# Two-layer transform kernel: the odd part accumulates onto the even part in one PSUM bank, VectorE forms only the difference, one round later

## The chip, the cores and the metric

One core of a Trainium2 chip runs the whole program. The metric is the device time of one execution in microseconds, from the first to the last instruction and the little that lies around it. Three executions of the kernel before gave 2941.29, 2942.25 and 2944.97 us, so the time to beat is the median, 2942.25 us. The engines are named as the profile names them: PE is TensorE's matmul (PEld its weight load), DVE is VectorE, ACT is ScalarE, POOL is GpSimd, SP is SyncE, whose queue issues most transfers.

## The reference

The input `x` is 8 x 3072 x 256. Three layers follow one another, cut here to what matters:

```
X = fft(fft(x, axis=1), axis=2).real          # 24576 tokens of width 256
h = X @ w_in            (256 -> 2048)
y = (h - tanh(h)) @ w_out   (2048 -> 256)
h2 = y @ w_in2          (256 -> 1024)
s = h2 * softmax(h2)
out = layernorm(s) * g_ln @ w_out2   (1024 -> 256)
```

All of it is float32.

## The kernel before, in words

A first stage (about the first 160 us) does the transform along the sequence and leaves, for each batch, an even part and an odd part in device memory. The transform along the width is folded into `w_in`: `fold_w_in` (L385 to L412) makes weights `wt` with two parts, one for the even and one for the odd part of a token. A token and its mirrored partner share these parts: with a = even part + (middle row) and b = odd part, the token's hidden value is a + b and the partner's is a - b. The middle row is one extra number per token, `nu`, kept in device memory as `nu_d`, with weights `wnu`. Row 0 of the odd part carries no data; `low` inside `fold_w_in` clears its weights with a memset on POOL (L410).

The main stage is a loop over steps (L1149), 48 groups of 512 tokens by 16 blocks of 128 hidden units, so 768 steps; the document calls a step a **round**. Each float32 product is three passes with split operands (high x high, high x low, low x high), so three matmuls. In round (n, m), before the change:

- PE: `ab` (L871) makes the even part and the odd part side by side in one PSUM tile `ab` (six matmuls of 256 columns), pool `p_ab`, two banks.
- DVE: `lead` (L886) makes `asb` = nu * wnu + even part; `act_in` (L893) then writes `asb` + odd part (L900) and `asb` - odd part (L901) into a PSUM tile `h` (pool `p_h`, one bank). ACT takes tanh of `h` into `t` (L907).
- One round later, `act_out` (L910): DVE subtracts, t = h - t (L912); ACT rounds the result to the high part `gh` and POOL takes the rest as its low part (helpers at L166 and L169, which also split `xs`, `ut` and `zs`).
- Two rounds later, `o1` (L919): six matmuls of 512 columns add `gh` times `w_out` into `x2p` (L927).

Interleaved with this, a second layer runs on pairs of 128-token tiles, one pair in eight rounds. `layer2` (L1095) keeps, for three places in a round ("ahead", "early", "late"), a list of works with the round in which each is due, counted from the pair's first round by `pair_at` (L1091). The document numbers these rounds **0 to 7**, one **period**. What matters here:

- Round 0, "ahead": PE makes a first block product in `bank_a`, ACT copies `bank_a` to `bank_b` (L1099). Round 0, "late": PE adds another product to `bank_a`, so it must wait for that copy.
- Round 1, "ahead": a product is added to `bank_b` and ACT keeps it in SBUF (`kept`, L971); "late": a further product is added to `bank_b`, after that copy.
- Round 4: products into `bank_b` (early) and `bank_a` (late). Round 5, "ahead": DVE takes `bank_a` with a running minimum (`block`, L978); "late": PE adds a further product to `bank_a`, after that read.
- Round 6: a DVE `block`. Rounds 7 and 0: the two `weigh` operations of DVE (L1002), with two SBUF inputs. Rounds 1 and 3: transposes through device memory (`turn`). Rounds 2, 3, 6 and 7: PE's output products `po` (`outp`), eight matmuls each.

The periods alternate, since a group has 16 rounds. In one, DVE forms four sums of blocks of the previous group (`sum_x2`, L943) in rounds 6 and 7: the **S-period** of this document. In the other, ACT and POOL split the next group's input `zs` near the same place: the **Z-period**. Both end with a round 0 and its copy. All engines work through their queues in the order of the program (`manual_schedule`); nothing reorders them.

## Time and profile before

| what | value |
|---|---|
| median of three executions | 2942.25 us |
| the profiled execution, its own time | 2943.85 us |
| its span, first to last instruction | 2942.1 us |
| PE busy / DVE busy / POOL busy / ACT busy | 93% / 88% / 77% / 71% |
| mean granted TensorE clock | 0.978 |
| DMA | 103 GB/s on average, 360 GB/s in the first slices |

The span is cut into stages by what runs there: the transform stage until about 160 us, the main loop until about 2900 us, and a tail of the last tiles. In the 40 slices of the page every engine has nearly the same busy share throughout the main loop. Times of single instructions are durations by the profiler; where two instructions follow on one engine, the document also uses the distance of their starts, since ends overlap. A remark like "[0.78 <-ACT bank_b L1099]" behind a row says that the engine idled 0.78 us just before, and what released it.

### The profile page before, as it was taken

What the parts mean: (1) busy time and instruction counts of PE and PEld (TensorE: products, weight loads), DVE (VectorE), ACT (ScalarE), POOL (GpSimd) and SP (SyncE); (2) the same over time, 40 slices, a digit from 0 to 9 for tenths busy, and PEclk for the clock granted to TensorE, in tenths of its full rate; (3) what the DMA queues carried; (4) which work ended last, traced back from release to release, by engine and by line L of the source; (5) the groups of instructions that cost most, each with busy time, mean ns of one, the idle gap of its engine ahead of it and who ended that gap; (6) DMA issues with size and microseconds to landing.
All of it is one profiled execution on the core that took longest, in us unless ns stands there. A gap on an engine that the chain in (4) does not pass through costs nothing.

```text
span 2942.1 us, 47965 instructions
## 1 busy us (share of the span) xinstructions
PE 2742.7 (93%) x15073; PEld 2364.6 (80%) x15073; DVE 2600.9 (88%) x4970; ACT 2098.6 (71%) x3990; POOL 2250.9 (77%) x2500
## 2 busy tenths in 40 slices
PE   9988999999999999999999999999999999999998
PEld 5667887888888788788888878888888888888887
DVE  8978898888988989888998889889888889888995
ACT  3556777777777777777777777777777777777776
POOL 0057887888888788888878888887887888888784
PEclk9999999999999999999999999999999999999999
DMA  9932333434334343443434434343443434334341
GB/s 360 362 117 47 91 94 85 101 83 98 85 89 100 84 95 86 94 94 81 100 85 96 93 85 96 85 95 87 92 95 84 101 82 98 87 87 101 82 97 47
DMA packets 882558, 302.97 MB, mean 103 GB/s; under 512 B 788496, under 2 KB 844048, under 8 KB 879008
## 3 DMA queue, kind: packets, MB, share of 16 engines
q1 hardware_dynamic: 879696, 293.40, 40.8%
q10 hardware_dynamic: 2304, 6.42, 0.6%
q8 instruction: 121, 1.98, 0.3%
...
## 4 chain that ended last, share of the span: by engine, by line
PE 37%; DVE 28%; POOL 14%; ACT 10%; issue 9%; DMA 2%; SPq 0%; POOLq 0%; DVEq 0%; ACTq 0%
PE x2p L927 12%; PE ab L877 7%; PE bank_a L956 5%; DVE asb L888 4%; DVE t L912 4%; DVE h L900 4%; DVE h L901 4%; PE bank_b L956 4%; DVE xb L943 3%; PE po L1060 3%; POOL ut L169 3%; DVE u L1002 3%; POOL gh L169 3%; DVE u L978 2%; POOL xs L169 2%
## 5 line engine op out<-in xcount | busy, mean ns | idle before, releaser
L927 PE MATMUL x2p<-gh,wo 128*128 128x512 f32 x4608 | 1150.4, 385 | 2.6 <-POOL gh L169 1.3
L169 POOL TENSOR_TENSOR gh<-t,gh 128x512 fp32r<-128x512 f32 x768 | 1000.3, 1305 | 130.4 <-ACT gh L166 113.5
L927 PEld LDWEIGHTS x2p<-gh,wo 128*128 128x128 f32 x4608 | 835.4, 192 | 141.5 <-POOL gh L169 35.9
L907 ACT ACTIVATE t<-h 128x512 f32<-128x512 f32 x758 | 452.9, 598 | 420.5 <-DVE h L901 322.0
L877 PEld LDWEIGHTS ab<-zs,wt 128*128 128x128 f32 x4608 | 650.4, 196 | 55.8 <-issue 12.1
L166 ACT ACTIVATE gh<-t 128x512 fp32r<-128x512 f32 x768 | 481.1, 626 | 264.0 <-DVE t L912 231.2
L877 PE MATMUL ab<-zs,wt 128*128 128x256 f32 x4608 | 656.6, 280 | 11.1 <-DVE bank_b L901 9.6
L912 DVE TENSOR_TENSOR t<-h,t 128x512 f32<-128x512 f32 x758 | 514.4, 679 | 107.5 <-ACT t L907 80.9
L169 POOL TENSOR_TENSOR ut<-um,ut 128x512 fp32r<-128x512 f32 x372 | 497.5, 1338 | 81.7 <-ACT ut L166 44.4
L1060 PE MATMUL po<-wo,ut 128*128 128x512 f32 x1528 | 523.1, 383 | 0.8 <-DVE x2t L169 0.8
L956 PE MATMUL bank_a<-wi,xs 128*128 128x512 f32 x1128 | 325.8, 399 | 151.2 <-ACT bank_b L1099 150.3
L888 DVE SCALAR_TENSOR_TENSOR asb<-nb,wnu,ab 128x256 f32<-128x256 f32 x768 | 364.7, 475 | 106.3 <-PE ab L877 88.7
L1067 PE MATMUL po<-wo,ut 128*128 128x256 f32 x1528 | 417.2, 273 | 0.0
L169 POOL TENSOR_TENSOR xs<-xb,xs 128x256 fp32r<-128x256 f32 (+1 forms) x282 | 241.4, 856 | 182.7 <-ACT xs L166 181.3
L956 PEld LDWEIGHTS bank_a<-wi,xs 128*128 128x128 f32 x1128 | 202.9, 193 | 210.5 <-ACT bank_b L1099 188.9
L901 DVE TENSOR_TENSOR h<-asb,ab 128x256 f32<-128x256 f32 x758 | 324.5, 428 | 26.1
L900 DVE TENSOR_TENSOR h<-asb,ab 128x256 f32<-128x256 f32 x758 | 324.6, 428 | 26.0
L1060 PEld LDWEIGHTS po<-wo,ut 128*128 128x128 f32 x1528 | 290.5, 190 | 31.6 <-DVE x2t L169 1.0
L1002 DVE SCALAR_TENSOR_TENSOR u<-u,e 128x1024 f32<-128x1024 f32 x188 | 312.9, 1664 | 0.0
L1067 PEld LDWEIGHTS po<-wo,ut 128*128 128x128 f32 x1528 | 293.9, 192 | 0.3 <-POOL ut L169 0.2
L956 PE MATMUL bank_b<-wi,xs 128*128 128x512 f32 x846 | 265.0, 412 | 18.6 <-POOL xs L169 7.5
L166 ACT ACTIVATE ut<-um 128x512 fp32r<-128x512 f32 x372 | 231.3, 622 | 23.5 <-DMA um<-mv_d 23.0
...
## 6 DMA issues: line engine op xcount, KB each, us to landing
...
```

What stands on the lines that cost most here:

```text
L166: nc.scalar.activation(out=o, in_=i, func=AF.Copy)
L169: eng.tensor_tensor(out=o, in0=i, in1=hi.bitcast(F32), op=ALU.subtract)
L877: nc.tensor.matmul(in_pairs(pab[:, u]), wt[c][:, hw, u, o : o + P], in_turn(zs[:, hz, u]), start=(i == 0), stop=(i == 2),)
L888: nc.vector.scalar_tensor_tensor(out=asb, in0=zg[n][1], scalar=wnu[:, m : m + 1], in1=pab[:, 0], op0=ALU.mult, op1=ALU.add)
L900: nc.vector.tensor_tensor(out=h[:, 0], in0=asb, in1=pab[:, 1], op=ALU.add)
L901: nc.vector.tensor_tensor(out=h[:, 1], in0=asb, in1=pab[:, 1], op=ALU.subtract)
L907: nc.scalar.activation(out=t, in_=h, func=AF.Tanh)
L912: nc.vector.tensor_tensor(out=g, in0=hs.pop((n, m)).rearrange("p u n -> p (u n)"), in1=g, op=ALU.subtract)
L927: nc.tensor.matmul(in_pairs(x2p[n][mt]), wo1[c][:, hw, k, mt * P : (mt + 1) * P], in_turn(gh[:, hg]), start=(m == 0 and i == 0), stop=(m = ...
L956: nc.tensor.matmul(in_pairs(bank), xs[:, hx, xs_at[a]], in_turn(wi2[:, b, hw]), start=(start and q == 0), stop=(q == 2), skip_group_check= ...
L1060: nc.tensor.matmul(in_pairs(po), ut[:, 0, ks], wo2[:, k].rearrange("p h x n -> p (x n) h"), start=(k == 0), stop=False,)
L1067: nc.tensor.matmul(in_pairs(po[:, :D]), ut[:, 1, ks], wo2[:, k, :, 0].rearrange("p h n -> p n h"), start=False, stop=(k == NK2 - 1),)
```

## The change

The odd part's row 0, empty before, now carries `nu` as data and keeps the weights of the middle row (the memset is gone). So the odd part's product contains nu * wnu. PE makes the even part into `h`'s first half, DVE makes `asb` = nu * wnu + even part from it, and only after that PE adds the odd part on top, in the same bank. The first half is then even + odd + nu * wnu, which is the token's value without a DVE operation, and DVE makes the partner's as 2 * asb - first half, with one scalar_tensor_tensor. `ab` and `p_ab` are gone; `p_h` has three banks in place of one. `parity(.., 1)` and `act_in` come one round after `even` and `lead`, so tanh, `act_out`, `o1` and all of the second layer come one round later too. For each of the 48 groups one DMA of 1 KB on SP brings `nu` into row 0 of `zc`.

```diff
         o = zc[n, u] = zp.tile([P, GP], F32, tag="zc", name=f"zc{n}_{u}")
         for _ in sums_of(eng, o, zf[:, u, 0], zf[:, u, 1], n % GPB - NSJ):
             pass
+        if u == 1:
+            b, g = divmod(n, GPB)
+            nc.sync.dma_start(out=o[0:1], in_=nu_d[b : b + 1, g * GP : (g + 1) * GP])
...
             yield rest(nc.vector, wt[c][:, 1], wf, wt[c][:, 0])
-            nc.gpsimd.memset(wt[c][0:1, :, 1].bitcast(F32), 0.0)
...
-    p_ab = pool(first, "p_ab", 2, space=PSUM)
-    p_h = pool(first, "p_h", 1, space=PSUM)
+    p_h = pool(first, "p_h", 3, space=PSUM)
...
+    def parity(n, m, u):
+        zs = zg[n][2]
         c, o = m // 4, (m % 4) * P
+        for i, (hw, hz) in enumerate(PASSES):
+            nc.tensor.matmul(
+                in_pairs(hs[n, m][:, 0]),
+                wt[c][:, hw, u, o : o + P],
+                in_turn(zs[:, hz, u]),
+                start=(u == 0 and i == 0),
+                stop=(i == 2),
+                skip_group_check=True,
+            )
+
+    def even(n, m):
+        if n == 0 and m % 5 > 2:
+            hs[n, m] = (bank_a, bank_b)[m % 5 - 3].rearrange("p (u n) -> p u n", u=2)
+        else:
+            hs[n, m] = p_h.tile([P, 2, GP], F32, tag="h", name=f"h{n}_{m}")
+        parity(n, m, 0)
...
-        nc.vector.tensor_tensor(out=h[:, 0], in0=asb, in1=pab[:, 1], op=ALU.add)
-        nc.vector.tensor_tensor(out=h[:, 1], in0=asb, in1=pab[:, 1], op=ALU.subtract)
+        h = hs[n, m]
+        nc.vector.scalar_tensor_tensor(
+            out=h[:, 1], in0=as_.pop((n, m)), scalar=2.0, in1=h[:, 0], op0=ALU.mult, op1=ALU.subtract
+        )
...
-        p, r = divmod(step - NM - 4 - back, 8)
+        p, r = divmod(step - NM - 5 - back, 8)
...
-    for step in range(steps + 2):
+    for step in range(steps + 3):
         n, j = divmod(step, NM)
         if step in at_ab:
             special(at_ab[step])
+        if 0 < step <= steps:
+            parity(*divmod(step - 1, NM), 1)
         if step < steps:
-            pab = ab(n, j)
-            asb = lead(n, j, pab) if n == 0 else None
-
-        lag = 2 if step < NM else 1
+            even(n, j)
+        if 0 < step <= steps:
+            act_in(*divmod(step - 1, NM))
+        lag = 3 if step < NM else 2
...
         layer2(step, "ahead")
         if step < steps:
-            act_in(n, j, pab, asb or lead(n, j, pab))
+            lead(n, j)
         if 0 < n < NG:
-            for blk in {2: (S1, S2, S3), 3: (S4,)}.get(j, ()):
+            for blk in {3: (S1, S2, S3), 4: (S4,)}.get(j, ()):
...
-        s1 = step - 4 if step < NM else step - 2
+        s1 = step - 5 if step < NM else step - 3
```

The order in which the engines get their work moves with it. DVE, rounds 6 and 7 of an S-period, in the kernel before (`t` is the result of `act_out`, `asb` of `lead`, `xb` the block sums, the ISA rows are `block`, `u71` with `e71` is `weigh`; a name's first two numbers are group and block):

```order
L912 TENSOR_TENSOR t19_1_13483<-h19_1_13480,t19_1_13483 128x512
L888 SCALAR_TENSOR_TENSOR asb19_2_13510<-nb19_12931,wnu_123,ab19_2_13499 128x256
L900 TENSOR_TENSOR h19_2_13512<-asb19_2_13510,ab19_2_13499 128x256
L901 TENSOR_TENSOR h19_2_13512<-asb19_2_13510,ab19_2_13499 128x256
L943 TENSOR_TENSOR xb_1232<-xb_1232 128x256 x3
L978 ISA u70_13309,st70_13310<-bank_a_1246,u70_13309,st70_13310 128x512
L978 ISA st70_13310 128x1
L912 TENSOR_TENSOR t19_2_13515<-h19_2_13512,t19_2_13515 128x512
```

And in the changed kernel:

```order
L901 SCALAR_TENSOR_TENSOR h19_2_12882<-asb19_2_12894,h19_2_12882 128x256
L913 TENSOR_TENSOR t19_1_12887<-h19_1_12850,t19_1_12887 128x512
L894 SCALAR_TENSOR_TENSOR asb19_3_12924<-nb19_12331,wnu_123,h19_3_12913 128x256
L944 TENSOR_TENSOR xb_1227<-xb_1227 128x256 x3
L979 ISA u70_12733,st70_12734<-bank_a_1241,u70_12733,st70_12734 128x512
L979 ISA st70_12734 128x1
L901 SCALAR_TENSOR_TENSOR h19_3_12913<-asb19_3_12924,h19_3_12913 128x256
L913 TENSOR_TENSOR t19_2_12918<-h19_2_12882,t19_2_12918 128x512
```

A round has three operations in place of four, and the round now begins with the difference, which needs this round's first matmuls; `t` of the block before stands behind it.

ACT, from the end of round 7 to the copy of round 0 (L1099 before, L1100 now), in the kernel before:

```order
L993 ACTIVATE e70_13564,st70_13310<-u70_13309,st70_13310 128x1024
L1077 ACTIVATE o2_68_13574<-po68_13525,st68_12984 128x512
L166 ACTIVATE xs_1233<-xb_1232 128x256
L166 ACTIVATE gh19_3_13598<-t19_3_13560 128x512
L1099 COPY bank_b_1247<-bank_a_1246 128x512
L907 ACTIVATE t19_4_13610<-h19_4_13607 128x512
```

And in the changed kernel:

```order
L994 ACTIVATE e70_12977,st70_12734<-u70_12733,st70_12734 128x1024
L1078 ACTIVATE o2_68_12987<-po68_12934,st68_12423 128x512
L166 ACTIVATE xs_1228<-xb_1227 128x256
L909 ACTIVATE t19_4_13005<-h19_4_12962 128x512
L166 ACTIVATE gh19_3_13008<-t19_3_12967 128x512
L1100 COPY bank_b_1242<-bank_a_1241 128x512
```

The tanh (`t` from `h`) moved from behind the copy to ahead of the rounding and the copy, in every round in which ACT copies a bank.

POOL, rounds 6 and 7 of a Z-period (`zs` the split of the next group's input), in the kernel before:

```order
L169 TENSOR_TENSOR gh19_9_13841<-t19_9_13819,gh19_9_13841 128x512
L1085 TENSOR_TENSOR o2_69_13754<-o2_69_13754 128x256
L169 TENSOR_TENSOR xs_1233<-xb_1232,xs_1233 128x256
L169 TENSOR_TENSOR gh19_10_13881<-t19_10_13849,gh19_10_13881 128x512
L169 TENSOR_TENSOR xs_1233<-xb_1232,xs_1233 128x256
L169 TENSOR_TENSOR zs20_13589<-zc20_0_13762,zs20_13589 128x256
L169 TENSOR_TENSOR zs20_13589<-zc20_1_13765,zs20_13589 128x256
```

And in the changed kernel:

```order
L169 TENSOR_TENSOR gh19_9_13240<-t19_9_13208,gh19_9_13240 128x512
L1086 TENSOR_TENSOR o2_69_13160<-o2_69_13160 128x256
L169 TENSOR_TENSOR xs_1228<-xb_1227,xs_1228 128x256
L169 TENSOR_TENSOR zs20_12958<-zc20_0_13118,zs20_12958 128x256
L169 TENSOR_TENSOR zs20_12958<-zc20_1_13121,zs20_12958 128x256
L169 TENSOR_TENSOR gh19_10_13282<-t19_10_13237,gh19_10_13282 128x512
L169 TENSOR_TENSOR xs_1228<-xb_1227,xs_1228 128x256
```

The split of `zs` is tied to the block number 11, everything of the second layer to the round; so `zs` now stands one round earlier against the second layer, ahead of the low part of `gh` of round 7.

## Rows read from the trace of the kernel before

**Rows 1.** PE's timeline, a Z-period's hold (start us, us, engine, line, operation, count)

```profile
1504.81 1.46 PE L927 MATMUL x2p<-gh,wo 128*128 128x512 f32 x6
1507.04 0.92 PE L956 MATMUL bank_a<-wi,xs 128*128 128x512 f32 x3 [0.78 <-ACT bank_b L1099]
1507.79 0.83 PE L877 MATMUL ab<-zs,wt 128*128 128x256 f32 x6
...
1509.11 1.46 PE L927 MATMUL x2p<-gh,wo 128*128 128x512 f32 x6
1510.41 0.81 PE L956 MATMUL bank_b<-wi,xs 128*128 128x512 f32 x3
```

**Rows 2.** PE's timeline, the next S-period's hold, and the next Z-period's

```profile
1527.31 0.83 PE L877 MATMUL ab<-zs,wt 128*128 128x256 f32 x6
...
1530.58 0.83 PE L877 MATMUL ab<-zs,wt 128*128 128x256 f32 x6
...
1531.90 1.46 PE L927 MATMUL x2p<-gh,wo 128*128 128x512 f32 x6
1535.71 0.92 PE L956 MATMUL bank_a<-wi,xs 128*128 128x512 f32 x3 [2.35 <-ACT bank_b L1099]
...
1563.48 0.91 PE L956 MATMUL bank_a<-wi,xs 128*128 128x512 f32 x3 [0.78 <-ACT bank_b L1099]
```

**Rows 3.** The instructions of line 1099: duration min/median/max, first and last start

```profile
L1099 ACT COPY bank_b<-bank_a x94: 576/580/678, 224.1 to 2871.8; 128x512 f32<-128x512 f32 x94
```

**Rows 4.** A window behind another hold: busy PE, PEld, DVE, ACT, POOL, granted clock, DMA

```profile
910.50:912.00 1.50, 1.50 (x7) 1.41 (x7) 1.44 (x4) 0.40 (x1) 1.50 (x1) 0.50 0.00 0
```

**Rows 5.** Waits of PEld: us in total, times, longest us

```profile
PEld bank_b L956 <- POOL xs L169: 37.7, 66, 1.0
...
PEld bank_b L956 <- ACT u L971: 15.0, 23, 1.6
```

**Rows 6.** DVE's timeline, rounds 6, 7 and 0 of the S-period

```profile
1526.35 2.71 DVE L943 TENSOR_TENSOR xb<-xb 128x256 f32<-128x256 f32 x3
1528.99 0.74 DVE L978 CUSTOM_DVE_ANT_0 u<-bank_a,u,st 128x512 f32<-128x512 f32 x1
...
1529.66 0.68 DVE L912 TENSOR_TENSOR t<-h,t 128x512 f32<-128x512 f32 x1
1530.26 0.47 DVE L888 SCALAR_TENSOR_TENSOR asb<-nb,wnu,ab 128x256 f32<-128x256 f32 x1
1530.76 0.43 DVE L900 TENSOR_TENSOR h<-asb,ab 128x256 f32<-128x256 f32 x1
1531.22 0.43 DVE L901 TENSOR_TENSOR h<-asb,ab 128x256 f32<-128x256 f32 x1
1531.56 1.14 DVE L943 TENSOR_TENSOR xb<-xb 128x256 f32<-128x256 f32 x1
1532.62 1.21 DVE L1002 SCALAR_TENSOR_TENSOR u<-u,e 128x1024 f32<-128x1024 f32 x1
...
1533.76 0.68 DVE L912 TENSOR_TENSOR t<-h,t 128x512 f32<-128x512 f32 x1
```

**Rows 7.** DVE's timeline in the Z-period: a `weigh`, and the first DVE operation behind PE's

```profile
1502.40 2.30 DVE L1002 SCALAR_TENSOR_TENSOR u<-u,e 128x1024 f32<-128x1024 f32 x1
...
1508.66 0.48 DVE L888 SCALAR_TENSOR_TENSOR asb<-nb,wnu,ab 128x256 f32<-128x256 f32 x1 [0.30 <-PE ab L877]
```

**Rows 8.** POOL's timeline, the same Z-period and the S-period's round 7

```profile
1500.47 0.73 POOL L1085 TENSOR_TENSOR o<-o 128x256 f32<-128x256 f32 x1
...
1502.34 1.28 POOL L169 TENSOR_TENSOR gh<-t,gh 128x512 fp32r<-128x512 f32 x1
1505.21 0.74 POOL L169 TENSOR_TENSOR xs<-xb,xs 128x256 fp32r<-128x256 f32 x1 [1.59 <-ACT xs L166]
1505.90 2.45 POOL L169 TENSOR_TENSOR zs<-zc,zs 128x256 fp32r<-128x256 f32 x2
...
1531.14 1.28 POOL L169 TENSOR_TENSOR gh<-t,gh 128x512 fp32r<-128x512 f32 x1 [1.49 <-ACT gh L166]
```

More of the change, by code (lines that the diff above doesn't have):

```diff
@@ L866, in fft2_moe_moe_kernel @@
     bank_b = p_pr.tile([P, HF], F32, tag="b", name="bank_b")
-    hs, ts_, gs = {}, {}, {}
+    hs, as_, ts_, gs = {}, {}, {}, {}
     x2p, x2s = {}, {}
-    def ab(n, m):
-        _, nb, zs = zg[n]
+    def parity(n, m, u):
+        zs = zg[n][2]
         c, o = m // 4, (m % 4) * P
-        pab = p_ab.tile([P, 2, GP], F32, tag="ab", name=f"ab{n}_{m}")
-        for u in range(2):
-            for i, (hw, hz) in enumerate(PASSES):
-                nc.tensor.matmul(
-                    in_pairs(pab[:, u]),
-                    wt[c][:, hw, u, o : o + P],
-                    in_turn(zs[:, hz, u]),
-                    start=(i == 0),
-                    stop=(i == 2),
-                )
-        return pab
@@ L886, in lead @@
-    def lead(n, m, pab):
-        asb = wk.tile([P, GP], F32, tag="asb", bufs=1, name=f"asb{n}_{m}")
+        for i, (hw, hz) in enumerate(PASSES):
[13 more added lines that the diff above has]
+        parity(n, m, 0)
@@ L888, in lead, with act_in @@
+    def lead(n, m):
+        asb = as_[n, m] = wk.tile([P, GP], F32, tag="asb", name=f"asb{n}_{m}")
         nc.vector.scalar_tensor_tensor(
[L889 removed]
+            out=asb, in0=zg[n][1], scalar=wnu[:, m : m + 1], in1=hs[n, m][:, 0], op0=ALU.mult, op1=ALU.add
         )
[L891 to L893 removed]
+    def act_in(n, m):
         b, g = divmod(n, GPB)
[L896 to L901 removed]
+        h = hs[n, m]
+        nc.vector.scalar_tensor_tensor(
+            out=h[:, 1], in0=as_.pop((n, m)), scalar=2.0, in1=h[:, 0], op0=ALU.mult, op1=ALU.subtract
+        )
@@ L905, in act_in @@
             )
-        t = wk.tile([P, 2, GP], F32, tag="t", bufs=4, name=f"t{n}_{m}")
+        t = ts_[n, m] = wk.tile([P, 2, GP], F32, tag="t", bufs=4, name=f"t{n}_{m}")
         nc.scalar.activation(out=t, in_=h, func=AF.Tanh)
-        hs[n, m], ts_[n, m] = h, t
     def act_out(n, m):
```

7 lines of the change are left out of this document (removed).

## The prediction

> **What bounds the kernel now.** I read the page first: PE 93% busy, DVE 88%, flat over the main loop. Two engines near full say that the loss lies in the waits between them, so I went to the waits, then to PE's timeline. There PE runs without a break for most of a period and stops at one place: the late product of round 0, which waits for ACT's copy of the bank [rows 1, 2]. The copy comes once a period; 94 copies from 224.1 to 2871.8 us give (2871.8 - 224.1)/93 = 28.47 us a period [rows 3], 56.94 for a pair of periods. There are 47 pairs.
>
> Prices on PE: 6 x 256 and 3 x 512 columns are equally many, and 1507.79 to 1509.11 is 1.32 us for both, so 0.66 each; six of 512 columns take 1.30 (1509.11 to 1510.41) [rows 1]. Rounds 6 and 7 take 3.27 us each (1527.31 to 1530.58) [rows 2]. The stop in the Z-period: last `x2p` due to end at 1504.81 + 1.30 = 1506.11, next product at 1507.04, hold 0.93. In the S-period: 1531.90 + 1.30 = 1533.20 against 1535.71, hold 2.51 [rows 1, 2]. After a wait, the three matmuls last 0.92 in place of 0.81, so each stop costs 0.11 more [rows 1].
>
> Why is the copy late? It stands on ACT behind the rounding of `gh`, and that behind DVE's subtraction. In the S-period DVE does the block sums (2.64 us) and the fourth sum and `weigh` (2.20) ahead of the subtraction that starts at 1533.76 [rows 6]. From that subtraction's end (1534.44) to PE's resumption (1535.71) it is 1.27 us: rounding, copy and handovers [rows 2, 6]. Smaller losses: PE waits for the split `xs` 37.7 us in all and for ACT's `kept` copy 15.0 us [rows 5], 0.80 and 0.32 us a pair; and after some of the long holds the granted clock is 0.50, TensorE's lower level of 1.2 GHz in place of 2.4 [rows 4]. A pair without such a stretch, 1507.04 to 1563.48, takes 56.44 [rows 1, 2], 0.50 less than the mean.
>
> **The change, part by part.** PE's matmuls stay 768 x 12 with equal columns; the memset and 48 small DMAs are priced at the end.
>
> DVE's round. Today, by distances of starts: subtraction 0.60, `lead` 0.50, sum 0.46, difference 0.34, total 1.90 [rows 6]. The changed round has difference, subtraction, `lead`. The trace has no scalar_tensor_tensor of this form: the tensor_tensor on the same operands lasts 0.43, `lead` 0.47 [rows 6]; I take the latter, as it is the same instruction, less the 0.09 by which a following independent start overlaps (0.43 against 0.34). So 0.38 + 0.60 + 0.38 = 1.36: 0.54 less a round. The Trainium skill ("VectorE: DVE Perf Modes", The DRAIN you can't avoid) says that the next operation does not start until the pipe is empty. By that the changed round would take 0.47 + 0.68 + 0.47 = 1.62 and save only 0.28, the S-period's hold would be some 0.5 longer than I find below and the kernel some 24 us slower than forecast; the trace has the overlap, and decides.
>
> But the round begins later. Today DVE's subtraction is first; now the difference is, and it needs the odd part: three matmuls, 0.33 us, and then 0.21 us to DVE (1508.66 - 1507.79 = 0.87 for the 0.66 us of six) [rows 1, 7]. So DVE starts at 0.54 of a round, and everything "ahead" waits for 0.54, the difference and the subtraction.
>
> *S-period's copy.* Count from the start of round 6; round 0 starts at 6.54, its late product is due 1.32 + 1.30 later, at 9.16. DVE: 0.54; round of 1.36 to 1.90; sums 2.64 to 4.54; `block` 0.67 (1528.99 to 1529.66) to 5.21. Round 7: difference 5.21, subtraction 5.59, `lead` 6.19, fourth sum 6.57. Now a race. POOL's low part of `gh` started 1531.14 - 1529.66 = 1.48 behind the start of the subtraction [rows 6, 8], here at 7.07. The fourth sum took 1.06 today, beside that POOL operation; alone I put it at 0.34, the spacing of the other 256-column operation, so `weigh` starts at 6.91, before POOL, and takes 1.14 (1532.62 to 1533.76) [rows 6]. Then difference 8.05, subtraction 8.43 to 9.11, PE resumes at 10.38: hold 1.22. ACT has an exponential, an output and `xs` ahead of its tanh there, so I take 1.4 against 2.51: **-1.1**. Bounds: POOL first costs its 1.28 [rows 8], giving about 2.6 (+0.1); shorter sums give down to 0.9 (-1.6).
>
> *Z-period's copy.* No sums: difference of round 7 at 3.27 + 0.54 = 3.81, `weigh` due at 5.17. POOL: `gh` at 0.92 + 1.48 = 2.40, then 1.28, an addition 0.73 and `xs` 0.70, so the first of two `zs` (2.45) starts at about 5.1 and blocks `weigh` until 6.3. (A `weigh` beside POOL lasted 2.30, with the 1.28 us of `gh` under it, against 1.14 [rows 6 to 8].) `weigh` to 7.5; copy done and PE ready at 7.5 + 0.38 + 0.68 + 1.27 = 9.8. POOL then has the second `zs` and the low part of `gh` of round 5, done at 7.5 + 1.22 + 1.28 = 10.0; the last two `x2p` matmuls of round 0 want it at 9.16 - 0.43 = 8.73. So about 1.2 is lost, by `gh` and not by the copy, against 0.93: **+0.3**. Bounds: 0.6 if `gh` is in time (-0.3), 1.8 if both `zs` go before `weigh` (+0.9).
>
> *Round 1, `kept`.* Shortest chain: 0.54 + 0.38 + 0.68 + 1.27 = 2.87 against 2.62 due: 0.25 + 0.11 in both periods, 0.72 a pair, less today's 0.32: **+0.4** (bounds +0.2 and +0.7).
>
> *Round 5, `block`.* Today DVE reads `bank_a` early. Now it comes after difference and subtraction, at 0.54 + 0.38 + 0.60 = 1.52, lasts 0.74 [rows 6] and hands over in 0.06 (as the copy); PE's late product is due at 0.66 + 1.30 = 1.96. Stop 0.36 + 0.11, twice: **+0.95** (with a difference of 0.43, +0.85). No cover is left here: PE has nothing else queued.
>
> *`xs` of round 4.* Its POOL part stands behind the statistics of a tile whose square ACT starts after `kept`; tanh (0.50 of ACT) now precedes `kept`, and the new stop in round 1 gives 0.36 more. The wait's mean is 37.7/66 = 0.57 [rows 5], so I let it go: **-0.8** (bounds -0.8, 0).
>
> *Clock.* With the hold down to 1.4 I let the half-clock stretches go: **-0.5** (bounds -0.5, 0).
>
> Sum: -1.1 + 0.3 + 0.4 + 0.95 - 0.8 - 0.5 = -0.75 a pair, x 47 = -35 us. Once: one more round of depth, +3.3; the odd row's DMA waits on SP for the sum and delays the splitting of groups 0 and 1 in a stage where DMAs are busy, 0 to 6, I take +2; in the loop the split comes four rounds later, so 13 us cover it, and what SP has queued behind (stores, the transposes' DMAs) waits for POOL's sums at most in every other period, with three to five rounds to spare. The memset's removal is worth nothing, no one waits for POOL there. Together -30 us on the profiled execution's 2943.85, so 2914; its time stands 1.6 above the median, so **2912** against 2942.25. The terms at their bounds span -1.6 - 0.3 + 0.2 + 0.85 - 0.8 - 0.5 = -2.15 (2846) to +0.1 + 0.9 + 0.7 + 1.0 = +2.7 (3074).
>
> **The rivals.** *POOL first.* The place is DVE's `weigh` in round 7 of the S-period; it decides by whether `weigh` starts before POOL's low part, 6.91 against 7.07, a margin of 0.16. If POOL wins, the hold is 2.6, and the clock stretches stay: +0.1 + 0.3 + 0.4 + 0.95 - 0.8 = +0.95, x 47 + 5 = +50: 2992. For it: the margin is thin, and a fourth sum of 0.50 suffices. Against: nothing on POOL is due at that moment. The Trainium skill ("SBUF — State Buffer", Who interferes with whom) says that VectorE and GpSimd hold the shared port pair for a whole instruction and the later one blocks; by that rule the order of two starts decides the whole 1.28, and the 2.30 against 1.14 agrees.
>
> *`xs` stays.* If the split's lateness comes from POOL's own queue and not from ACT, the -0.8 falls away: +0.05 x 47 + 5: 2949, close to no change.
>
> *VectorE was the bound.* If the freed time goes through fully, both holds fall to the shortest chain, 0.25: -2.26 - 0.68 + 0.4 + 0.95 - 0.8 - 0.5 = -2.9, x 47 + 5 = -131: 2811. Against: the chains of round 7 and the sums are still there.
>
> *It doesn't do what it says.* The difference reads and writes one bank; at double length (0.9) each of three chains a period is 0.43 longer: +2.6 a pair, 121 us more than forecast, 3033. No row shows such a price.
>
> **How the numbers follow.** Forecast (2880 to 2937 with its terms half way to their bounds): 0.43. `xs` stays: 0.19. POOL first, with the double length: 0.27. VectorE the bound: 0.11. A measurement here tells 0.2%, 5.9 us, from no change. Faster: 0.43, 0.11 and a third of the `xs` case: 0.60. Same: half of the `xs` case and little else: 0.11. Slower: 0.29. The range leaves out most of the 2811 case and the upper half of the slower one: 2842 to 2992.
>
> **What would show it.** Right: DVE busy down by about 768 x 0.38 = 290 us; S-period holds before the late product of round 0 near 1.4; new idle before `bank_a` in round 5, released by `block`, near 0.36; the wait on `kept` in every period; no wait for `xs`. Wrong: holds of 2.5 or more in the S-period with `weigh` of over 2 us; no stop in round 5; or waits of the odd part for `lead`, which I put at nothing, since `lead` of round 7 ends at 6.19 + 0.47 = 6.66 against 6.54, inside the hold that follows.

## The result and the profile after

The changed kernel takes **2862.91 us** (median; 2861.21 to 2864.70) against 2942.41 for the kernel before in the same session: ratio 0.973, 95% interval 0.971 to 0.975. The forecast was 2912 with a range of 2842 to 2992: the sign is right and the time lies in the range, but the gain is 79 us where 30 were forecast. The profiled execution took 2864.70, its span is 2862.5.

The page of the changed kernel, its busy times and two groups (busy us, mean ns of one | idle before them, releaser):

```profile
PE 2734.3 (96%) x15073; PEld 2314.1 (81%) x15073; DVE 2109.5 (74%) x4202; ACT 2068.9 (72%) x3990; POOL 2343.0 (82%) x2496
...
L928 PE MATMUL x2p<-gh,wo 128*128 128x512 f32 x4608 | 1155.4, 384 | 52.1 <-POOL gh L169 51.8
...
L901 DVE SCALAR_TENSOR_TENSOR h<-asb,h 128x256 f32<-128x256 f32 x762 | 326.1, 428 | 686.2 <-PE h L876 685.5
```

DVE fell from 88% to 74% busy; two operations a round became the one of the second group, and one such is worth 762 x 0.428 = 326 us. POOL's share rose from 77% to 82%, with four instructions fewer: it now does some of the waiting that DVE did before (below; its `gh` lasts 1.40 us in the mean, 1.30 before). The first group is new: PE waits 51.8 us for POOL's `gh`.

The once-a-period copy, answering to [rows 3], and the mean granted clock (0.978 before):

```profile
L1100 ACT COPY bank_b<-bank_a x94: 577/581/602, 228.1 to 2791.9; 128x512 f32<-128x512 f32 x94
...
core 0: 2862.5 us, clock 0.994
```

(2791.9 - 228.1)/93 = 27.57 us a period, 55.14 a pair where it was 56.94: -1.80 a pair, x 47 = -85 us. The main loop carries the whole change; 4 us more stand ahead of the first copy (224.1 to 228.1), near the 5 that the prediction added once.

To see where, I took from PE's timeline, 300 to 2730 us, every gap between matmul blocks beyond the matmuls' own length, by its place in the period, and averaged each place over the 39 to 42 periods of a kind. A stop of round 5 is counted with the 0.11 behind it, as in the forecast. In us a pair:

| place | before | after | change | forecast |
|---|---|---|---|---|
| hold of round 0, S-period | 2.57 | 0.85 | -1.7 | -1.1 |
| hold of round 0, Z-period | 0.98 | 0.19 | -0.8 | +0.3 |
| round 1 (`kept`), half-clock stretches, the 0.11 behind each hold | 1.5 | 0.8 | -0.7 | -0.1 |
| round 4, `xs` | 0.83 | 0.06 | -0.8 | -0.8 |
| round 5, `block` | 0.09 | 0.94 | +0.85 | +0.95 |
| round 4, POOL's `gh` | 0 | 1.37 | +1.4 | none |
| sum | | | -1.8 | -0.75 |

The waits of the changed kernel (us in all, times, longest), answering to [rows 5]; PE's and PEld's show one stop from two sides:

```profile
PEld x2p L928 <- POOL gh L169: 106.4, 179, 1.8
PEld bank_a L957 <- DVE st L979: 54.3, 93, 0.7
PEld bank_b L957 <- ACT u L972: 38.7, 94, 0.8
...
PEld bank_b L957 <- POOL xs L169: 2.0, 5, 0.9
```

`xs` fell from 37.7 to 2.0. `kept` (`ACT u`) rose from 23 times to 94, every period. The release by `st` is round 5's `block`, 93 times. PE's timeline, answering to [rows 1, 2]: round 4 with its new stop, round 5, then the Z-period's round 0 and round 1, then the S-period:

```profile
1509.55 1.03 PE L928 MATMUL x2p<-gh,wo 128*128 128x512 f32 x4
1511.68 0.70 PE L928 MATMUL x2p<-gh,wo 128*128 128x512 f32 x2 [1.10 <-POOL gh L169]
...
1513.53 1.46 PE L928 MATMUL x2p<-gh,wo 128*128 128x512 f32 x6
1515.14 0.92 PE L957 MATMUL bank_a<-wi,xs 128*128 128x512 f32 x3
...
1523.76 1.55 PE L928 MATMUL x2p<-gh,wo 128*128 128x512 f32 x6
1525.20 0.92 PE L957 MATMUL bank_a<-wi,xs 128*128 128x512 f32 x3
...
1527.27 1.46 PE L928 MATMUL x2p<-gh,wo 128*128 128x512 f32 x6
1528.69 0.92 PE L957 MATMUL bank_b<-wi,xs 128*128 128x512 f32 x3
...
1550.22 1.66 PE L928 MATMUL x2p<-gh,wo 128*128 128x512 f32 x6
1552.34 0.92 PE L957 MATMUL bank_a<-wi,xs 128*128 128x512 f32 x3 [0.46 <-ACT bank_b L1100]
...
1555.83 0.92 PE L957 MATMUL bank_b<-wi,xs 128*128 128x512 f32 x3
```

Six `x2p` take 1.30. So round 5 stops from 1514.83 to 1515.14 (0.31), the Z-period's round 0 from 1525.06 to 1525.20 (0.14), round 1 from 1528.57 to 1528.69 (0.12), the S-period's round 0 from 1551.52 to 1552.34 (0.82). In round 4 the last two `x2p` come at 1511.68 where 1509.55 + 4 x 0.217 = 1510.42 was due: 1.26.

DVE's timeline, answering to [rows 6, 7]: the Z-period's `weigh`, then rounds 6, 7 and 0 of the S-period:

```profile
1521.02 1.68 DVE L1003 SCALAR_TENSOR_TENSOR u<-u,e 128x1024 f32<-128x1024 f32 x1
...
1544.21 2.30 DVE L944 TENSOR_TENSOR xb<-xb 128x256 f32<-128x256 f32 x3
1546.43 0.74 DVE L979 CUSTOM_DVE_ANT_0 u<-bank_a,u,st 128x512 f32<-128x512 f32 x1
...
1547.10 0.42 DVE L901 SCALAR_TENSOR_TENSOR h<-asb,h 128x256 f32<-128x256 f32 x1
1547.43 0.68 DVE L913 TENSOR_TENSOR t<-h,t 128x512 f32<-128x512 f32 x1
...
1548.76 1.22 DVE L1003 SCALAR_TENSOR_TENSOR u<-u,e 128x1024 f32<-128x1024 f32 x1
...
1550.24 0.68 DVE L913 TENSOR_TENSOR t<-h,t 128x512 f32<-128x512 f32 x1
```

POOL's timeline, answering to [rows 8]: round 4's queue, the Z-period's, and the low parts of `gh` beside the S-period's sums and `weigh`:

```profile
1507.92 1.00 POOL L169 TENSOR_TENSOR xs<-xb,xs 128x384 fp32r<-128x384 f32 x1
1508.89 1.51 POOL L272 TENSOR_TENSOR zc<-zf 128x128 f32<-128x128 f32 x4
1510.36 2.49 POOL L169 TENSOR_TENSOR gh<-t,gh 128x512 fp32r<-128x512 f32 x2
...
1520.87 2.44 POOL L169 TENSOR_TENSOR zs<-zc,zs 128x256 fp32r<-128x256 f32 x2
1523.27 1.28 POOL L169 TENSOR_TENSOR gh<-t,gh 128x512 fp32r<-128x512 f32 x1
...
1544.70 1.53 POOL L169 TENSOR_TENSOR gh<-t,gh 128x512 fp32r<-128x512 f32 x1 [0.57 <-POOL ut L169]
...
1548.91 2.21 POOL L169 TENSOR_TENSOR gh<-t,gh 128x512 fp32r<-128x512 f32 x1 [1.12 <-issue]
```

Read the two engines together. In the S-period `weigh` starts 0.15 us before `gh` and lasts 1.22; `gh`, 1.28 by itself, lasts 2.21. In the Z-period `weigh` starts 0.15 behind the first `zs`, waits for its end and lasts 1.68; the second `zs` waits for `weigh`, so that the pair lasts 2.44. And in round 4 POOL's four sums `zc`, 1.47 us from start to start, now stand ahead of the `gh` for which PE waits. They are issued at a fixed place of a group of 16 rounds (`j == 7`), and since the second layer runs one round later they now meet its round 2 where they met round 3.

On ACT, the rounding ahead of the S-period's copy starts 0.25 us behind the end of DVE's subtraction (1550.24 + 0.68 = 1550.92):

```profile
1551.17 0.62 ACT L166 ACTIVATE gh<-t 128x512 fp32r<-128x512 f32 x1
```

Some rows of the kernel before, for the readings further down. PE, from the late product of round 0 to that of round 1, behind two holds of the S-period (the second hold is that of [rows 2]); then the `weigh` beside the two `zs` of [rows 8], and POOL's `gh` under the three sums of [rows 6]:

```profile
909.01 1.23 PE L956 MATMUL bank_a<-wi,xs 128*128 128x512 f32 x3 [2.35 <-ACT bank_b L1099]
...
914.04 0.81 PE L956 MATMUL bank_b<-wi,xs 128*128 128x512 f32 x3
...
1539.46 0.92 PE L956 MATMUL bank_b<-wi,xs 128*128 128x512 f32 x3 [0.23 <-ACT u L971]
...
1506.53 1.22 DVE L1002 SCALAR_TENSOR_TENSOR u<-u,e 128x1024 f32<-128x1024 f32 x1
...
1526.42 1.49 POOL L169 TENSOR_TENSOR gh<-t,gh 128x512 fp32r<-128x512 f32 x1 [0.20 <-ACT gh L166]
```

### The profile page after: what moved, and what is told of

It is laid out like the page before. It is cut to its first block, busy times and chain, and to the rows that moved or that the text cites. A ratio compares the mean times of both kernels' runs of the same rounds, so it can differ in the third digit from the quotient of the medians.

```text
span 2862.5 us, 46875 instructions
## 1 busy us (share of the span) xinstructions
PE 2734.3 (96%) x15073; PEld 2314.1 (81%) x15073; DVE 2109.5 (74%) x4202; ACT 2068.9 (72%) x3990; POOL 2343.0 (82%) x2496
## 5 line engine op out<-in xcount | busy, mean ns | idle before, releaser
L169 POOL TENSOR_TENSOR gh<-t,gh 128x512 fp32r<-128x512 f32 x768 | 1073.5, 1401 | 254.2 <-ACT gh L166 116.0
L928 PE MATMUL x2p<-gh,wo 128*128 128x512 f32 x4608 | 1155.4, 384 | 52.1 <-POOL gh L169 51.8
L901 DVE SCALAR_TENSOR_TENSOR h<-asb,h 128x256 f32<-128x256 f32 x762 | 326.1, 428 | 686.2 <-PE h L876 685.5
L876 PEld LDWEIGHTS h<-zs,wt 128*128 128x128 f32 x4572 | 628.3, 191 | 51.9 <-DVE asb L894 11.5
L876 PE MATMUL h<-zs,wt 128*128 128x256 f32 x4572 | 637.2, 275 | 5.4 <-DVE asb L894 5.3
L169 POOL TENSOR_TENSOR ut<-um,ut 128x512 fp32r<-128x512 f32 x372 | 477.5, 1284 | 9.3 <-ACT ut L166 9.3
L894 DVE SCALAR_TENSOR_TENSOR asb<-nb,wnu,h 128x256 f32<-128x256 f32 x762 | 359.7, 472 | 0.3 <-PE h L876 0.3
L169 POOL TENSOR_TENSOR xs<-xb,xs 128x256 fp32r<-128x256 f32 (+1 forms) x282 | 277.7, 985 | 0.2
L1003 DVE SCALAR_TENSOR_TENSOR u<-u,e 128x1024 f32<-128x1024 f32 x188 | 274.8, 1461 | 0.0
L957 PE MATMUL bank_b<-wi,xs 128*128 128x512 f32 x846 | 240.2, 392 | 4.0 <-ACT u L972 3.4
L1033 DVE STREAM_TRANSPOSE tb<-u 128x1024 f32<-128x1024 f32 x186 | 230.2, 1238 | 0.0
```

What stands on the lines that cost most here:

```text
L169: eng.tensor_tensor(out=o, in0=i, in1=hi.bitcast(F32), op=ALU.subtract)
L876: nc.tensor.matmul(in_pairs(hs[n, m][:, 0]), wt[c][:, hw, u, o : o + P], in_turn(zs[:, hz, u]), start=(u == 0 and i == 0), stop=(i == 2), ...
L894: nc.vector.scalar_tensor_tensor(out=asb, in0=zg[n][1], scalar=wnu[:, m : m + 1], in1=hs[n, m][:, 0], op0=ALU.mult, op1=ALU.add)
L901: nc.vector.scalar_tensor_tensor(out=h[:, 1], in0=as_.pop((n, m)), scalar=2.0, in1=h[:, 0], op0=ALU.mult, op1=ALU.subtract)
L928: nc.tensor.matmul(in_pairs(x2p[n][mt]), wo1[c][:, hw, k, mt * P : (mt + 1) * P], in_turn(gh[:, hg]), start=(m == 0 and i == 0), stop=(m = ...
L957: nc.tensor.matmul(in_pairs(bank), xs[:, hx, xs_at[a]], in_turn(wi2[:, b, hw]), start=(start and q == 0), stop=(q == 2), skip_group_check= ...
```

## The experiments

Theory A: the holds shrank because DVE's rounds 6, 7 and 0 got shorter and `weigh` beats POOL by 0.15 us; what the change gives back comes from places in queues (the z sums ahead of `gh` on POOL, `block` and `kept` behind the new difference). Rival B: the second layer's lateness lies on POOL or ACT, and DVE's freed time has little to do with it. Each run was compared with the kernel before on the same chip (2944.55, 2946.91 and 2946.51 us). The table under the last experiment has the gaps of all of them.

**1. z sums one round later.**

```
-                if j == 7:
+                if j == 8:
                     sum_z(n + 1, u, nc.gpsimd)
```

> The changed kernel with GpSimd's sums for the next group's input issued one round later (round 3 of a period in place of round 2), so that they stand behind the low part of gh as in the kernel before. Theory A (the 1.1 us wait of x2p for gh in round 4 of every second period comes from these sums being queued ahead of gh): the wait goes, 1.3 us a pair of periods times 47 = about -60 us, near 2800. Rival B (GpSimd is simply too full at 82%, the wait moves to another round): no gain, 2850 to 2865.

Measured: 2801.20 us (2800.16 to 2806.24), ratio 0.9515, interval 0.9491 to 0.9538, 62 us below the changed kernel. This is A's number. POOL's timeline and PE's wait of this run:

```profile
1476.56 1.29 POOL L169 TENSOR_TENSOR gh<-t,gh 128x512 fp32r<-128x512 f32 x1
1477.81 1.51 POOL L272 TENSOR_TENSOR zc<-zf 128x128 f32<-128x128 f32 x4
```

```profile
PE x2p L928 <- POOL gh L169: 2.4, 11, 0.6
```

The wait of 51.8 us is 2.4: `gh` stands ahead of `zc` again. The change had given away 62 us at a line that it does not touch.

**2. The second layer's "ahead" part in front of the difference.** This undoes the part of the change by which `block` and `kept` stand behind difference and TanH.

```
-        if 0 < step <= steps:
-            act_in(*divmod(step - 1, NM))
         lag = 3 if step < NM else 2
...
         layer2(step, "ahead")
+        if 0 < step <= steps:
+            act_in(*divmod(step - 1, NM))
```

> The changed kernel with the subtraction of the round before and all 'ahead' work of the second layer put in front of the difference and tanh on VectorE and ScalarE, as in the kernel before. Theory A (the stops of round 5, 0.47 us, and of round 1, 0.28 us, in every period exist because block and the kept copy queue behind the difference, which needs this round's matmuls): both go, 1.5 us a pair = -70 us; up to 0.8 us a pair may come back where TensorE waits for xs in round 4, since the kept copy again precedes tanh: 2770 to 2830. Rival B (these stops only hide the next wait on the same chain): 2850 to 2870.

Measured: 2806.95 (2806.40 to 2808.04), ratio 0.9530, interval 0.9512 to 0.9548, in A's range. The stops of rounds 1 and 5 and the Z-period's hold are gone; the S-period's hold rose to 1.35, since `weigh` there now lasts 2.21: it comes second to POOL. The wait for `xs` did not come back, though `kept` again precedes tanh on ACT:

```profile
PEld bank_b L957 <- POOL xs L169: 5.0, 11, 1.3
```

**3. One more DVE operation a round** (a 256-column sum behind `lead`, into the half of the bank that is overwritten later; the result is unused).

```
             lead(n, j)
+            nc.vector.tensor_tensor(out=hs[n, j][:, 1], in0=zg[n][1], in1=hs[n, j][:, 0], op=ALU.add)
```

> The changed kernel with one more VectorE operation per round, behind lead: a sum of the removed one's kind and size into the half of the bank that the difference overwrites later; so VectorE works as long as before the change, and the order stays. Theory A (the gain is VectorE's freed time on the path through rounds 6, 7 and 0 of the periods with block sums, and weigh starting before GpSimd's low part there): 0.34 to 0.46 us on two rounds, and weigh behind GpSimd, 1 to 2.3 us a pair: +47 to +108 us, 2910 to 2970. Rival B (the gain is the moved order of ScalarE's and GpSimd's queues; VectorE now idles 686 us for TensorE, so an operation more is hidden): within 15 us of 2863.

Measured: 2969.19 (2968.26 to 2970.17), ratio 1.0081, interval 1.0062 to 1.0100: the gain is gone, at the top of A's range. The S-period's hold is 1.92. But the operation also reads the bank, so PE's odd part waits for it (38.2 us in all), some 0.8 a pair in round 7. So this run shows that DVE's round is worth that much here, not that the hold alone is. Nor is it the whole of DVE's old work: DVE is busy for 2411.8 us, against 2600.9 in the kernel before, and the hold is 1.92 and not 2.57. What makes the other 0.65 is not shown by it.

**4. Only the race:** 256 columns of memset, once a pair, ahead of the fourth sum.

```
             for blk in {3: (S1, S2, S3), 4: (S4,)}.get(j, ()):
+                if blk == S4:
+                    nc.vector.memset(hs[n, j][:, 1], 0.0)
                 sum_x2(blk)
```

> The changed kernel with one small memset of 256 columns on VectorE, about 0.3 us, ahead of the fourth block sum, once in every second period. Theory A (weigh wins the shared port by 0.15 us: it starts at 1548.76 and GpSimd's low part at 1548.91): weigh now starts behind GpSimd and waits for it, the hold of round 0 grows from 0.85 by 0.3 and about 1.2 us more: +1.2 to +1.6 us a pair, +55 to +75 us, or more if the granted clock falls again behind the longer hold. Rival B (no race: VectorE and GpSimd share the port): only the 0.3 us, +14 us.

Measured: 2922.77 (2921.25 to 2925.73), ratio 0.9924, interval 0.9905 to 0.9944: 60 us for a memset of 0.27 us, 47 times. DVE's and POOL's timelines of this run:

```profile
1578.39 0.27 DVE L1172 MEMSET h<- 128x256 f32 x1
1578.57 0.41 DVE L944 TENSOR_TENSOR xb<-xb 128x256 f32<-128x256 f32 x1
1578.89 2.31 DVE L1003 SCALAR_TENSOR_TENSOR u<-u,e 128x1024 f32<-128x1024 f32 x1
```

```profile
1578.67 1.45 POOL L169 TENSOR_TENSOR gh<-t,gh 128x512 fp32r<-128x512 f32 x1 [1.12 <-issue]
```

Now `gh` starts 0.22 before `weigh`, `weigh` lasts 2.31 in place of 1.22, and the hold is 1.90 in place of 0.85. The Trainium skill ("SBUF — State Buffer", Who interferes with whom) says that of VectorE and GpSimd the one that comes later to the shared port waits for the other's whole instruction; the two rows agree, 1.09 longer by 0.37 us in the order of starts. Rival B falls for the S-period's hold.

**5. Only round 5's `block` first in its round.**

```
-                (5, lambda p: block(2 * p + 1, 1, bank_a, True, False)),
             ),
+            "first": ((5, lambda p: block(2 * p + 1, 1, bank_a, True, False)),),
...
+        layer2(step, "first")
         if 0 < step <= steps:
             act_in(*divmod(step - 1, NM))
```

> Only the block of round 5 is put ahead of the difference on VectorE. Theory A (the block waits 0.36 us behind the difference and the late product behind the block, and the 0.11 us stop after it follows from it): the idle time before bank_a in round 5 goes in both periods, 0.94 us per pair, 47 pairs: 44 us less than the changed kernel's 2863, so about 2819 (2805 to 2835). Rival B (the stop only moves: the difference 0.6 us later makes TanH, gh and the products two rounds on late): 2850 to 2875, with a new stop elsewhere.

Measured: 2870.68 (2868.26 to 2872.61), ratio 0.9740, interval 0.9724 to 0.9756: A's 44 us did not come, and B's range held: the stop moved. Round 5's stop is gone, and its 0.94 stands elsewhere: 0.79 before PE's odd part (most of it at the end of round 7) and 0.2 more in the S-period's hold. DVE's timeline, POOL's and PE's of this run, rounds 6 to 0 of an S-period:

```profile
1493.44 3.27 DVE L944 TENSOR_TENSOR xb<-xb 128x256 f32<-128x256 f32 x3
...
1498.23 0.47 DVE L894 SCALAR_TENSOR_TENSOR asb<-nb,wnu,h 128x256 f32<-128x256 f32 x1
```

```profile
1492.84 1.28 POOL L169 TENSOR_TENSOR ut<-um,ut 128x512 fp32r<-128x512 f32 x1
1494.15 1.40 POOL L169 TENSOR_TENSOR gh<-t,gh 128x512 fp32r<-128x512 f32 x1
```

```profile
1498.75 0.94 PE L876 MATMUL h<-zs,wt 128*128 128x256 f32 x6 [0.46 <-DVE asb L894]
```

The three sums take 3.27 where the changed kernel's take 2.30: without the stop PE and DVE reach them earlier against POOL's queue, and `ut` and `gh` run under them. `asb` comes late by that, and PE waits for it. The stop in round 5 had paid for itself. (This is read from the rows; no run moves POOL's queue alone.)

**6. Experiments 1 and 2 together.**

```
-                if j == 7:
+                if j == 8:
                     sum_z(n + 1, u, nc.gpsimd)
...
-        if 0 < step <= steps:
-            act_in(*divmod(step - 1, NM))
         lag = 3 if step < NM else 2
...
         layer2(step, "ahead")
+        if 0 < step <= steps:
+            act_in(*divmod(step - 1, NM))
```

> Both edits together: z sums one round later, and the second layer's ahead part in front of the difference. Theory A (the stops have separate causes, so they add): the 1.55 us of round 4 that the second edit alone left in one period of each pair goes as well, 47 x 1.55 = 73 us from 2807, about 2734 (2715 to 2760), with round 0 of that period still holding some 1.35. Rival B (one queue is short whatever the order, and the stop moves on): 2780 or more.

Measured: 2853.41 (2849.78 to 2859.20), ratio 0.9686, interval 0.9672 to 0.9700: far from A's 2734, in B's range, and slower than either edit alone. The hold of the Z-period is back at 1.68. DVE's timeline and POOL's at one of them:

```profile
1399.88 4.78 DVE L1003 SCALAR_TENSOR_TENSOR u<-u,e 128x1024 f32<-128x1024 f32 x1
```

```profile
1399.52 0.73 POOL L169 TENSOR_TENSOR xs<-xb,xs 128x256 fp32r<-128x256 f32 x1
1400.21 1.44 POOL L169 TENSOR_TENSOR zs<-zc,zs 128x256 fp32r<-128x256 f32 x2
1401.61 1.28 POOL L169 TENSOR_TENSOR gh<-t,gh 128x512 fp32r<-128x512 f32 x1
1402.85 0.73 POOL L169 TENSOR_TENSOR xs<-xb,xs 128x256 fp32r<-128x256 f32 x1
```

`weigh` begins under the first `xs` and gets nowhere until POOL has a gap, after five instructions. So it went in 34 of 45 Z-periods. The two edits are not independent: each moves POOL's queue against DVE's.

**7. z sums later, and the items of rounds 1 and 5 first in their rounds.**

```
-                if j == 7:
+                if j == 8:
                     sum_z(n + 1, u, nc.gpsimd)
...
-                (1, lambda p: (product(p, bank_b, S2, T2), new_u(2 * p), kept(2 * p, 1))),
-                (5, lambda p: block(2 * p + 1, 1, bank_a, True, False)),
             ),
+            "first": (
+                (1, lambda p: (product(p, bank_b, S2, T2), new_u(2 * p), kept(2 * p, 1))),
+                (5, lambda p: block(2 * p + 1, 1, bank_a, True, False)),
+            ),
...
+        layer2(step, "first")
         if 0 < step <= steps:
             act_in(*divmod(step - 1, NM))
```

> z sums one round later, and only round 1's kept copy and round 5's block in front of difference and TanH; round 0 stays as in the changed kernel. Theory A: from 2801 the stops of round 5 (0.94 per pair) and round 1 (0.54 per pair) go, 70 us: about 2731 (2715 to 2750), the hold of round 0 staying 0.85 and 0.26. Rival B (VectorE or ScalarE is late elsewhere then): 2765 or more.

Measured: 2876.08 (2869.30 to 2892.57), ratio 0.9769, interval 0.9735 to 0.9804: slower than the first experiment by 75 us, and in B's range. The sums take 3.26, the odd part waits 0.75, and a stop for `xs` is back in round 4, 0.7 in both periods. The Z-period's hold is 0.77 in the mean: its `weigh` starts 0.04 to 0.12 us behind the first `zs` and lasts 3.7 to 4.4 us in 11 of 44 periods, at most 1.78 in the others.

**8. z sums later, and the whole "ahead" part first.**

```
-                if j == 7:
+                if j == 8:
                     sum_z(n + 1, u, nc.gpsimd)
...
+        layer2(step, "ahead")
         if 0 < step <= steps:
             act_in(*divmod(step - 1, NM))
...
-        layer2(step, "ahead")
```

> z sums one round later, and the whole ahead part (round 0's copy, round 1's kept copy, round 5's block) in front of difference, TanH and gh. Theory A (the hold of round 0 is ACT's copy standing behind gh, which waits for VectorE): as the copy no longer stands behind gh, the holds of 0.85 and 0.26 and the 0.1 after each go too, some 1.3 per pair, 60 us below 2731: about 2671 (2655 to 2715). Rival B (TanH and gh behind the copy come late two rounds on, and the late part of the S-period's round 0 stops for them instead): 2720 to 2780.

Measured: 2827.23 (2826.50 to 2828.92), ratio 0.9596, interval 0.9582 to 0.9610. That is above both ranges. The holds did go down, to 0.41 and 0.17, as A says of a copy that no longer stands behind `gh`. The stops of round 4 and of the odd part take more than that: 1.79 and 0.79.

From here Theory C ascribed the stop in round 4 to `kept` and the one in round 7 to `block`, each standing ahead of difference and TanH; rival D is stated with each run.

**9. z sums later, and round 1's `kept` alone first.**

```
-                if j == 7:
+                if j == 8:
                     sum_z(n + 1, u, nc.gpsimd)
...
-                (1, lambda p: (product(p, bank_b, S2, T2), new_u(2 * p), kept(2 * p, 1))),
...
+            "first": ((1, lambda p: (product(p, bank_b, S2, T2), new_u(2 * p), kept(2 * p, 1))),),
...
+        layer2(step, "first")
         if 0 < step <= steps:
             act_in(*divmod(step - 1, NM))
```

> z sums one round later, and only round 1's product and kept copy in front of difference and TanH; the block of round 5 stays behind. Theory C (in the run with both in front, the stop of 0.7 us for xs in round 4 comes from the kept copy, which makes ScalarE wait for the product before TanH, and the stop of 0.66 in round 7 from the block): here round 1's 0.54 per pair goes, round 4's 0.7 comes in both periods, round 7 has none: 2801 - 25 + 66 = 2842 (2825 to 2855). Rival D (both new stops come from the block alone): only the 25 us go, 2776 (2765 to 2790).

Measured: 2854.60 (2852.34 to 2857.26), ratio 0.9695, interval 0.9680 to 0.9709. The stops are where Theory C puts them, and the time is at the top of its range: round 1's stop goes, none comes in round 7, and `xs` is late in every period. The wait for `xs`, and ACT's `kept` in one of the periods:

```profile
PEld bank_b L957 <- POOL xs L169: 80.9, 93, 1.6
...
1523.43 0.59 ACT L972 COPY u<-bank_b 128x512 f32<-128x512 f32 x1 [1.81 <-PE bank_b L957]
```

It was 2.0 us in the changed kernel and 37.7 before. Here `kept` stands ahead of tanh and of `gh`, and ACT idles 1.81 us for the product in front of both. The order of `kept` and tanh alone does not make `xs` late: experiment 2 has `kept` ahead of tanh, behind `gh`, and its wait is 5.0 us.

**10. z sums later, and round 5's `block` between difference and subtraction.**

```
-                if j == 7:
+                if j == 8:
                     sum_z(n + 1, u, nc.gpsimd)
...
-                (5, lambda p: block(2 * p + 1, 1, bank_a, True, False)),
             ),
+            "first": ((5, lambda p: block(2 * p + 1, 1, bank_a, True, False)),),
...
             act_in(*divmod(step - 1, NM))
+        layer2(step, "first")
         lag = 3 if step < NM else 2
```

> z sums one round later, and the block of round 5 between the difference and the subtraction that follows it on VectorE (before: behind both). Theory C (a block in front of the difference costs because VectorE stands before it for TensorE's product, and the difference and asb with it; behind the difference it holds up only the subtraction, which has a round to spare): round 5's 0.94 per pair goes and round 7 gets no stop, 2801 - 44 = 2757 (2745 to 2775). Rival D (asb is what comes late, wherever in front of it the block stands): a stop of 0.3 to 0.7 in round 7, 2775 to 2835.

Measured: 2840.15 (2839.59 to 2841.71), ratio 0.9646, interval 0.9632 to 0.9660. Theory C is wrong on `block`: it no longer stands ahead of the difference, and the sums still take 3.40 and the odd part waits 1.15 a pair. D's sign holds (the time is 5 us above its range), by what the rows of experiment 5 show: it is the sums beside POOL, not the order of `block` and difference.

**11. z sums later, and the whole "ahead" part between the two.**

```
-                if j == 7:
+                if j == 8:
                     sum_z(n + 1, u, nc.gpsimd)
...
             act_in(*divmod(step - 1, NM))
+        layer2(step, "ahead")
         lag = 3 if step < NM else 2
...
-        layer2(step, "ahead")
```

> z sums one round later, and the whole ahead part (copy of round 0, product and kept copy of round 1, block of round 5) between difference and TanH on the one side and subtraction and gh on the other. Theory C: as in the run with the block alone, and round 0's copy no longer stands behind gh, so that the holds of 0.85 and 0.26 go too unless VectorE's weigh loses the port to POOL: 2700 to 2745. Rival D (subtraction and gh behind the waits come late): 2775 to 2835.

Measured: 2821.54 (2819.89 to 2823.38), ratio 0.9582, interval 0.9568 to 0.9596, in D's range: the sums take 3.41 again, and the odd part waits 1.09.

**12. As the sixth, with the z sums two rounds later in place of one.**

```
-                if j == 7:
+                if j == 9:
                     sum_z(n + 1, u, nc.gpsimd)
...
-        if 0 < step <= steps:
-            act_in(*divmod(step - 1, NM))
         lag = 3 if step < NM else 2
...
         layer2(step, "ahead")
+        if 0 < step <= steps:
+            act_in(*divmod(step - 1, NM))
```

> The second layer's ahead part in front of the difference, and the z sums two rounds later instead of one. Theory C (the weigh that started just ahead of POOL's run of four instructions and waited for all of them took the gain of the run with one round later; where it falls against POOL is decided by a few tenths of a us, so another shift of POOL can move it out): weigh before the hold about 1.2 to 1.7 in the period that splits z, that hold below 0.3, round 4 without its stop: 2734 (2715 to 2775). Rival D (the z sums out of round 2 starve it wherever they go): holds of 1.3 and 1.7 again, 2835 to 2865.

Measured: 2842.00 (2833.96 to 2854.75), ratio 0.9666, interval 0.9639 to 0.9693: holds of 1.31 and 1.61, `weigh` held for about 5 us in 27 of 44 Z-periods. D holds for this place: two rounds later does not move it out either.

All of them, gaps of PE in us a pair, then the mean length of the three sums and of the S-period's `weigh` (us). "Odd part" is every wait before the odd part, rounds 6 to 0:

| kernel | time | S hold | Z hold | round 4 | round 5 | odd part | sums | `weigh` |
|---|---|---|---|---|---|---|---|---|
| before | 2942 | 2.57 | 0.98 | 0.83 | 0.09 | 0 | 2.70 | 1.21 |
| the change | 2863 | 0.85 | 0.19 | 1.43 | 0.94 | 0 | 2.30 | 1.21 |
| 1 | 2801 | 0.85 | 0.26 | 0.07 | 0.93 | 0.02 | 2.30 | 1.21 |
| 2 | 2807 | 1.35 | 0 | 1.61 | 0.02 | 0 | 2.76 | 2.21 |
| 3 | 2969 | 1.92 | 0.20 | 1.44 | 0.87 | 1.07 | 2.71 | 2.27 |
| 4 | 2923 | 1.90 | 0.16 | 1.36 | 0.91 | 0.26 | 2.30 | 2.28 |
| 5 | 2871 | 1.05 | 0.25 | 1.60 | 0 | 0.79 | 3.26 | 1.21 |
| 6 | 2853 | 1.32 | 1.68 | 0.29 | 0.08 | 0 | 2.77 | 2.18 |
| 7 | 2876 | 1.07 | 0.77 | 1.67 | 0.10 | 0.75 | 3.26 | 1.21 |
| 8 | 2827 | 0.41 | 0.17 | 1.79 | 0.10 | 0.79 | 3.26 | 1.21 |
| 9 | 2855 | 0.85 | 0.15 | 1.74 | 0.86 | 0.04 | 2.32 | 1.21 |
| 10 | 2840 | 1.05 | 0.45 | 0.14 | 0.15 | 1.15 | 3.40 | 1.21 |
| 11 | 2822 | 0.55 | 0.39 | 0.94 | 0.18 | 1.09 | 3.41 | 1.21 |
| 12 | 2842 | 1.31 | 1.61 | 0.34 | 0 | 0 | 2.73 | 2.16 |

The sums are the same work in every row, between 2.30 and 3.41 us; so is `weigh`. The first experiment is the fastest kernel found, 4.9% below the kernel before.

## Why the prediction was right in sign and off in size

Its mechanism held: the S-period's copy comes earlier because DVE's round is shorter, and the price is paid in rounds 1 and 5. In the Z-period it forecast a loss by `gh` that did not come. What failed were the sizes of three terms (the two holds and the clock), and one term was missing. Against the forecast the sum is 1.05 us a pair lower: about -0.6 and -1.1 from the two holds, -0.6 from round 1 and the clock, -0.1 from round 5, +1.4 from round 4. That the time lies in the range is luck: the missing term hid 62 us of the error, and without it (experiment 1) the kernel takes 2801, below the range's 2842.

- *DVE's round.* Right. The difference lasts 0.428 and the next operation starts 0.33 behind it (1547.10 to 1547.43): 0.38 was taken. The other price there, 1.62 a round, did not come. The section of the Trainium skill that it was taken from ("VectorE: DVE Perf Modes", The DRAIN you can't avoid) adds that a next operation that is not held starts earlier, which the prediction left out; the trace agrees with that, 0.33 from start to start for an operation of 0.42.
- *S-period's copy, -1.1; measured -1.7.* The step that failed is "sums 2.64 to 4.54": the old length was kept for the sums. They take 2.22 (1544.21 to 1546.43), as less of POOL's queue runs under them: its `gh` starts 0.49 behind the first sum (1544.70), where it started 0.07 behind (1526.42 against 1526.35 [rows 6]). That is 0.42. The 0.18 allowed for ACT was nearly right: from the subtraction's end to PE it is 1.42 (1550.92 to 1552.34) where 1.27 was walked. The rest, 0.13, is DVE's other steps, each walked a little too long. The race came out as walked: a margin of 0.16 forecast, 0.15 measured, and experiment 4 shows that it decides.
- *Z-period's copy, +0.3; measured -0.8.* The step that failed is "the first of two `zs` blocks `weigh` until 6.3". It took half of the 2.45 of [rows 8] for each `zs`; but that pair too had been stretched by a `weigh` (1506.53, between the two). One by itself lasts 0.7 (two in 1.44, experiment 6). So `weigh` waited to 5.7 and not 6.3, ended at 6.74 (1522.63 - 1515.89), and `gh` was done at 8.66, in time for 8.73. Only the copy was then late, by 0.14. This is read from the rows; no run tests it alone.
- *Round 1, +0.4, and clock, -0.5; measured -0.7 together.* From the late product of round 0 to that of round 1 PE takes 3.37 where nothing stops it (1507.04 to 1510.41 [rows 1], and so behind every Z-period's hold of the kernel before). Behind its S-period's holds it took 3.75 in 13 of 42 pairs, with a stop of 0.39 for `kept` (1535.71 to 1539.46), and 4.8 to 5.05 in the other 29, at the lower clock (909.01 to 914.04, with the 0.50 of [rows 4]). The mean is 4.61. In the changed kernel it is 3.54 and 3.53, the stop of round 1, and nothing longer than 3.95. So the stop of round 1 went from some 0.15 a pair to 0.55 with its 0.11: +0.4 was right. The term that was mis-sized is the clock's: the stretches cost 1.1 a pair, not 0.5. The pair that gave the 0.5 has none of them, but it has the stop for `kept` that the others don't.
- *Round 5, +0.95.* Right: a stop of 0.94. But its stop also spaced DVE's sums from POOL's queue, so that removing it gained nothing (experiment 5): the term was right and "no cover is left" was not the whole account.
- *`xs`, -0.8.* Right in size. The reason given, that tanh now precedes `kept` and round 1 has a stop, is not shown: experiment 9 takes away both and makes `xs` late, but ACT also idles there, and experiment 2 takes away both and `xs` stays in time.
- *Missing: z sums on POOL, +1.4.* The prediction followed the odd row's DMA and said that 13 us cover it, but did not look at what the POOL sums themselves now stand in front of. One more round of depth moves the second layer past all that is set by `j`; I listed the DMAs and the split, not the four `zc`. It cost 62 us.
- *The rivals.* "POOL first" did not happen, and its price was fair: 1.28 put, 1.05 measured on the hold in experiment 4. "VectorE was the bound" was the nearest on the holds, -2.5 together where it said -2.9 and the forecast -0.8; without the stop of round 4 the kernel goes below its 2811 (2801, experiment 1). "`xs` stays" and "it doesn't do what it says" fell.
- *What would show it.* DVE busy fell by 491 us, not 290. The sums account for 50 of it (179.1 to 128.7) and `weigh` for 38 (312.9 to 274.8), both beside POOL. The other 403 are 0.53 a round, which is the 0.54 that the prediction itself had found for the round; its 290 used the 0.38 of one operation.

Still open: why the combined orders (6, 12) starve `weigh` so often, and whether some place for the sums and for `zs` keeps both holds and round 5 short at once.
